# Inverse length-64 Fourier step as four 64x64 tiles from the second batch on

## The chip, the cores and the metric

The kernel runs on one core of a Trainium2 chip. The metric is the device time of one execution in microseconds; lower is better. The engines are named as in the profile: PE (TensorE: matmuls; its weight loads stand apart as PEld), DVE (VectorE), ACT (ScalarE), POOL (GpSimd) and SP (SyncE, which here only issues DMAs).

## The reference

Eight batches of 3008 rows (sequence) by 256 channels. First a filter in the frequency domain along the sequence, then an MLP mixer: over the sequence (tokens) and over the channels.

```python
X = np.fft.rfft(x, axis=1)                       # x: (8, 3008, 256)
y = np.fft.irfft(X * (filt_r + 1j * filt_i)[None], n=3008, axis=1)
h = np.maximum(y.transpose(0, 2, 1) @ w_tok1, 0.0) @ w_tok2   # 3008 -> 256 -> 3008
u = y + h.transpose(0, 2, 1)
out = u + np.maximum(u @ w_ch1, 0.0) @ w_ch2     # 256 -> 1536 -> 256
```

All data is fp32; the weights of the mixer arrive as float64 and are converted on the chip in the first part of the run.

## The kernel before

3008 is 47 x 64, and the length-3008 transform is done in two stages: one over the 64 rows that lie 47 apart, one over the 47. Rows n1 and -n1 are handled together (A = 24 pairs), so that each stage works with sums and differences. The first stage writes `z_tmp` to DRAM, the second reads it turned, multiplies with the filter and goes back over the 47, and leaves `g_tmp` in DRAM. What remains is the inverse over the 64: a product of each piece of `g_tmp` (tile `t4`, 128 partitions: 32 frequencies by 4 parts) with the constant table `wai` (128 x 128). This last step is not done by itself. It is accumulated into the same PSUM banks as the second token product, so that the bank holds u = y + h at once: `u_filter` (line 876) issues 4 matmuls of 128 columns with `t4` as the stationary operand and `wai` moving, for each half dh of the channels.

The mixer (`mix`) walks over items (b, m, jp): batch b, column block m (MT = 6 blocks of 512 sequence positions, the last of 448) and jp (JP = 6, pairs of 128 of the 1536 hidden channels). The two channel products, the second token product and, from the second batch on, the first token product use a Strassen-Winograd scheme: 7 products of half size in place of 8, with sums formed on DVE. A block of an item:

- place 0: `up_first` (L977: 4 matmuls into the two banks `ps_pg`), `up_middle` (DVE sums `hh` and `s`), `h_sums` of the item before (DVE `t`), part 0 of `down` (L1011), parts of the next u;
- place 1: `up_last` (L993: 3 matmuls; DVE `hh` twice, ACT relu twice), then up to two steps from the list `todo_v`;
- place 1.5 and 2: parts 1 and 2 of `down`, the steps of `finish` (DVE, then 16 output DMAs on POOL), parts of the next u.

The next block's u is made in four parts by `u_quarter` (L898 for the seven products, banks `ps_acc` and `ps_b` in turn): part 0 in item jp=2, part 1 at the begin of jp=3, parts 2 and 3 at its end; parts 2 and 3 begin with `u_filter`. Afterwards `v_steps` puts the channel sums (`v`: three DVE operations in two steps) into `todo_v`. For the first block of the next batch all of this lies in jp=4 and jp=5 of block m=5: parts 2 and 3 at place 0 of jp=5, the first two steps of `todo_v` at place 1, the rest at place 2. Batch 0 makes its u with `u_unit` and `u_filter`, with no Strassen scheme.

The forward filter of the next batch runs beside the mixer, at places that a table in the code fixes. From the third batch on it runs already as sets of four 64x64 matmuls (`four`, L528) on the four quarters of the array. DVE forms `sd` (x sums, L553), `p` (filter products, L709) and their join (L714, L715) for it.

The weights of the second token product, `w2`, lie in SBUF while batch 0 runs. `w2_sums` (POOL) forms the Strassen sums of each block during batch 0 and writes 7 matrices of 128 x 256 per block to `w2_tmp`; from batch 1 on `w2m_load` (SP) brings one block at a time back into one of two places.

The order on each engine is the order in which the code issues; nothing is rescheduled. Tiles with one or two buffers and the PSUM banks are what one engine waits for another for.

The lines that the steps below name:

```python
own = ({(3, 0): (0,), (3, 2): (1,)}, {(2, 2): (0,), (3, 0): (1,), (3, 2): (2, 3)})
new = {(JP - 2, 0): (0, 1), (JP - 1, 0): (2, 3)}
...
todo_v.extend(v_steps(b, m))
...
while todo_v and m + 1 == MT:
    one_step()
```

Of the kernel before, what the change touches and what calls it, by code (L numbers as in the profile page):

```python
# [59 lines left out]
def _make_tables():  # L60
# [12 lines left out]
    wa, wai = wa.reshape(P, P), wai.reshape(P, P)  # L73
# [51 lines left out]
    return wa.astype(f), np.concatenate((wa[one], wa[one])).astype(f), wa0.astype(f), wai.astype(f), wbi.astype(f), wbi0.astype(f)  # L125
# [3 lines left out]
def kernel(  # L129
# [13 lines left out]
    wa_np, was_np, wa0_np, wai_np, wbi_np, wbi0_np = _make_tables()  # L143
    wa_d = nc.inline_tensor(wa_np, name="wa_t").ap()
    was_d = nc.inline_tensor(was_np, name="was_t").ap()
    wai_d = nc.inline_tensor(wai_np, name="wai_t").ap()
    ident_d = nc.inline_tensor(np.eye(P, dtype=np.float32), name="ident_t").ap()
    wait_d = nc.inline_tensor(np.ascontiguousarray(wai_np.T), name="wait_t").ap()
# [7 lines left out]
                 for g, bs in enumerate(GROUPS)] for what, shape in (("z", (P, A)), ("g", (K2, KR))))  # L156

    w2_d = nc.dram_tensor("w2_tmp", (MT, P, 7, 256), FP32, kind="Internal").ap()
# [51 lines left out]
    w2m = [w2[:, t, 0:7 * 256].rearrange("p (s n) -> p s n", s=7) for t in range(2)]  # L210
# [145 lines left out]
    def w2_load(i):  # L356

        t, g = divmod(i, W2G)
        nn = min(NG, N2 - g * NG)
        n = nn * N1  # L360

        st = stage(512)
        nc.gpsimd.dma_start(st[:, 0:n], moe_w_tok2[ts(t, P), ds(g * NG * N1, n)])
        yield
        dst = w2[:, t].rearrange("p (a h n2) -> p h n2 a", h=2, n2=HALF)[:, :, ds(g * NG, nn), :]

        def some(h, first, step, w):
            return (lambda v: bass.AP(tensor=v.tensor, offset=v.offset + first, ap=[v.ap[0], [N1, nn], [step, w]]),
                    dst[:, h, :, 0:w])

        parts = [some(0, A - 1, -1, A), some(1, A, 1, A - 1)]
        if i < BY_PE:
            h = halves(st, n, spare_pair())
            yield next(h)
            yield next(h)
            on_chip(ident, *next(h), n, parts)
        else:
            yield from rounded(st, n, parts, False)
# [142 lines left out]
    def rows_of(t_d, b):  # L521
        g, i = place_of[b]
        return t_d[g].rearrange("k (g a) b d -> (k g) a b d", a=A)[:, :, i, :]
# [42 lines left out]
    def dft(bs):  # L566
# [109 lines left out]
        def bi_unit(k):  # L676


            ps = bank(free_bank()).rearrange("p (b d) -> p b d", b=2)[:, 0:nb, :]
            for i, p in enumerate(prods.pop(k)):  # L680
                wi = turn_i[:, k // WC % 4, k % WC] if i else wbs[k // WC][:, TI:TI + 2 * KR:2, k % WC]
                nc.tensor.matmul(ps[0:KR], wi, p, start=(i == 0), stop=(i == 1))
            c, r = divmod(k, KC)
            if r == 0:
                where, tag = (p2p, "p2") if c % 3 == 2 else (t3p, "t3")
                t3s[c] = where.tile([KR, KC, nb, D], FP32, tag=tag, name="t3")
            by_block(t3s[c][:, r], ps[0:KR])
            if r == KC - 1:
                nc.scalar.dma_start(g_d[0][ts(c, KC)].rearrange("k r b d -> r k b d"), t3s.pop(c))
# [27 lines left out]
        def bi_sets(c, tags):  # L717
# [7 lines left out]
            for h in range(2):  # L725
                nc.sync.dma_start(g_d[place_of[bs[0]][0]][ts(c, KD), ts(h, KH)].rearrange("k r b d -> r k (b d)"),
                                    t3[half_of(h, KH)])
# [53 lines left out]
    def t4_load(b, c, lo=PARTS[0], hi=P, queue=nc.sync):  # L781
        if lo == 0:
            t4[b, c] = t4p.tile([P, TC4, D], FP32, tag="t4", name="t4")
        queue.dma_start(t4[b, c][lo:hi], rows_of(g_d, b)[lo:hi, ts(c, TC4), :])
# [47 lines left out]
    def token_product(b):  # L832
# [20 lines left out]
        h1 = w2[:, 0:1, 7 * 256:].rearrange("p o (s t) -> p o s t", t=P)[:, :, 0:7, :]  # L853

        def finish_h1():
            v(c[:, 5:7], two[:, 1:3], c[:, 3:5])
            for at, to in ((slice(1, 7, 5), slice(0, 5, 4)), (slice(5, 8, 2), slice(1, 7, 5))):
                nc.scalar.activation(out=h1[:, 0, to, :], in_=c[:, at], func=AF.Relu)
# [29 lines left out]

    def u_quarter(b, m, h1, ut, i):

        w = width(m)
        hw = w // 2
        ps = bank(free_bank())
        if i >= 2:
            u_filter(b, m, i - 2, ps, True)
        todo = (((0, 0), (5, 3)), ((6, 4), (4, 6)), ((1, 1), (2, 2)), ((3, 5),))[i]
        for j, (n, at) in enumerate(todo):
            nc.tensor.matmul(ps[:, ds(j * hw, hw)], h1[:, n, :], w2m[m % 2][:, at, 0:hw],  # L898
                             start=(i < 2 and j == 0), stop=(j == len(todo) - 1))
        p0, p1 = ps[:, 0:hw], ps[:, hw:w]  # L900
        c11, c21, c22 = ut[:, 0, 0:hw], ut[:, 1, 0:hw], ut[:, 1, hw:w]
# [4 lines left out]
        elif i == 1:  # L906

            row = ut[:, 0, hw:w]
            both = bass.AP(tensor=row.tensor, offset=row.offset, ap=[row.ap[0], [512 - hw, 2], [1, hw]])
            v(both, ps[:, 0:w].rearrange("p (s n) -> p s n", s=2), c22.unsqueeze(1).to_broadcast([P, 2, hw]))  # L910
            v(c22, p0, c21)
        else:
            v(ut[:, i - 2, 0:w], ps[:, 0:w], ut[:, i - 2, 0:w])

    def w2m_load(m):
        hw = width(m) // 2
        nc.sync.dma_start(w2m[m % 2][:, :, 0:hw], w2_d[m, :, :, 0:hw])

    def w2_sums(m):

        w = width(m)
        hw = w // 2
        r = w2[:, :, ds(m * 512, w)]
        b11, b12, b21, b22 = (r[:, t, ds(j * hw, hw)] for t in range(2) for j in range(2))
        sub = lambda out, in0, in1: nc.gpsimd.tensor_tensor(out=out, in0=in0, in1=in1, op=ALU.subtract)

        def raw_out():
            nc.gpsimd.dma_start(w2_d[m, :, 0, 0:hw], b11)
            nc.gpsimd.dma_start(w2_d[m, :, 1:3, 0:hw], r[:, 1, :].rearrange("p (s n) -> p s n", s=2))

        def t13():
            sub(b22, b22, b12)
            sub(b12, b12, b11)

        def t24():
            nc.gpsimd.tensor_tensor(out=b11, in0=b22, in1=b11, op=ALU.add)
            sub(b21, b11, b21)

        def sums_out():
            for t in range(2):  # L940
                nc.gpsimd.dma_start(w2_d[m, :, ds(3 + 2 * t, 2), 0:hw], r[:, t, :].rearrange("p (s n) -> p s n", s=2))

        return [raw_out, t13, t24, sums_out]
# [70 lines left out]
    def store_piece(b, m, blocks, h, e, n, queues):  # L1014
        ob = out[b]
        cw = DH * CW
        row = e * 32 * N1 + (A + 4 * m if h else A - 1 - 4 * m)
        for g, q in enumerate(queues):
            q.dma_start(bass.AP(tensor=ob.tensor, offset=ob.offset + row * D + g * cw,  # L1019
                                ap=[[N1 * D, 32], [D if h else -D, n], [1, cw]]),  # L1020
                        blocks[ts(g, CW), h, e, 0:n])

    def last_item(b, m, jp, hh, t, ut, po):
# [29 lines left out]
        blocks = r.rearrange("p (q h e) d i -> p h e q (d i)", h=2, e=2)  # L1053
        for h in range(2):
            n = min(4, (w - h * HALF + HALF) // P)
            for e in range(2):
                for dh in range(DH):
                    rows = ut[:, dh].rearrange("p (q h e i) -> p h e q i", h=2, e=2, i=CW)
# [3 lines left out]
    def finish(b, m, ut, po):  # L1062
# [29 lines left out]
        def store():  # L1092
            turn(1)
            blocks = r.rearrange("p (q h e) d i -> p h e q (d i)", h=2, e=2)
# [30 lines left out]
    def mix(next_ready):  # L1125
# [14 lines left out]
        def u_parts(b, m, jp, place):  # L1140
# [5 lines left out]
            if now and now[-1] == max(p for ps in parts.values() for p in ps):  # L1146
                if m:
                    wait.append(m)
                todo_v.extend(v_steps(b, m))
# [92 lines left out]
    with tc.manual_schedule():  # L1242
        nc.sync.dma_start(wa0, wa0_d)
        nc.vector.memset(turned[:, A:K2, :], 0.0)
        for t in filts:
# [125 lines left out]
```

## Time and profile before

| | |
|---|---|
| median of 3 runs | 2401.5 us (2401.21 to 2401.79) |
| profiled execution: its span | 2400.3 us, so 1.2 us of the median lie around the span |
| PE busy | 2361.7 us, 98% |
| DVE busy | 1950.1 us, 81% |
| ACT busy | 689.6 us, 29% |
| POOL busy | 639.2 us, 27% |
| mean granted TensorE clock | 0.995 of full speed |
| DMA moved | 294.28 MB, mean 123 GB/s |

Busy time is the sum of the durations of an engine's instructions. Matmuls are pipelined: a row lasts longer than the distance to the next one, so for PE the starts of successive rows are what counts. DVE rows overlap a little as well. "Idle before, releaser" tells how long an engine stood idle ahead of a row and what ended this.

### The profile page before, as it was taken

The numbers are of one execution on the slowest core, as the hardware profiler recorded it, in microseconds if no ns is written. First come the engines' busy times: TensorE is split into PE (matmuls) and PEld (weight loads), VectorE is DVE, ScalarE is ACT, GpSimd is POOL, SyncE is SP. The second block draws the span as 40 slices with busy tenths as digits, with TensorE's granted clock in tenths as the row PEclk, the third lists the DMA queues.
The fourth block names the chain that finished last, engine by engine and source line by source line (L and its number), as shares of the span: only waits on it lengthen the run. The fifth ranks groups of instructions, "written<-read, shape, count | busy, mean of one in ns | idle before, by whom it ended". The sixth has DMA issues, their size and how long they took to land.

```text
span 2400.3 us, 37048 instructions
## 1 busy us (share of the span) xinstructions
PE 2361.7 (98%) x13132; PEld 2013.7 (84%) x13132; DVE 1950.1 (81%) x3669; ACT 689.6 (29%) x1339; POOL 639.2 (27%) x1124
## 2 busy tenths in 40 slices
PE   7989999999999999999999999999999999999998
PEld 4667788888898888988888888988889888898887
DVE  7798887788887888788887788788887788877786
ACT  5733222222223222232222222122222322212222
POOL 7475624211211121112111311221121112112121
PEclk8999999999999999999999999999999999999999
DMA  9964446333353333533344333533335433331100
GB/s 217 247 191 125 157 127 218 120 107 91 112 174 129 101 99 108 196 113 98 102 146 158 110 94 103 191 115 107 92 114 172 134 96 98 108 130 32 39 14 21
DMA packets 189719, 294.28 MB, mean 123 GB/s; under 512 B 34444, under 2 KB 124962, under 8 KB 189534
## 3 DMA queue, kind: packets, MB, share of 16 engines
q1 hardware_dynamic: 148046, 231.24, 30.8%
q0 software_dynamic: 34688, 53.83, 8.5%
q10 hardware_dynamic: 6800, 6.85, 0.9%
q8 instruction: 104, 1.70, 0.3%
q14 instruction: 81, 0.66, 0.1%
HBM read 209.06 MB, written 82.72 MB: 122 GB/s over the span
## 4 chain that ended last, share of the span: by engine, by line
PE 91%; DMA 3%; DVE 3%; POOL 1%; issue 1%; ACT 0%; SPq 0%; DVEq 0%; ACTq 0%; POOLq 0%
PE ps_po L1011 35%; PE ps_pg L977 19%; PE ps_pg L993 15%; PE ps_b L528 3%; PE ps_b L841 3%; PE ps_acc L898 3%; PE ps_acc L841 2%; PE ps_b L898 2%; PE ps_pg L528 2%; PE ps_b L876 2%; PE ps_acc L876 2%; PE ps_b L790 1%; DMA filt<-in_filt_r_dram 1%; DMA x<-in_x_dram 1%; DVE t L955 0%
## 5 line engine op out<-in xcount | busy, mean ns | idle before, releaser
L1019 POOL DMA_DIRECT2D out_dram<-r x752 | 408.3, 550 | 1454.0 <-issue 865.1
L998 ACT ACTIVATE hh<-hh 128x512 f32<-128x512 f32 (+1 forms) x576 | 347.9, 621 | 1015.8 <-DVE hh L955 1012.0
L955 DVE TENSOR_TENSOR hh<-ps_pg,s 128x512 f32<-128x512 f32 (+3 forms) x864 | 482.6, 586 | 168.1 <-ACT s L980 157.9
L1011 PE MATMUL ps_po<-t,wc 128*128 128x256 f32 (+1 forms) x2296 | 558.4, 380 | 0.8 <-DVE t L955 0.6
L1011 PEld LDWEIGHTS ps_po<-t,wc 128*128 128x128 f32 x2296 | 427.0, 190 | 96.4 <-issue 38.3
L977 PE MATMUL ps_pg<-v,wc 128*128 128x256 f32 (+1 forms) x1728 | 412.6, 375 | 0.1
L1011 PE MATMUL ps_po<-hh,wc 128*128 128x256 f32 (+1 forms) x1722 | 411.6, 375 | 0.6 <-POOL wc L387 0.6
L977 PEld LDWEIGHTS ps_pg<-v,wc 128*128 128x128 f32 x1728 | 328.2, 190 | 37.9 <-POOL wc L386 0.8
L1011 PEld LDWEIGHTS ps_po<-hh,wc 128*128 128x128 f32 x1722 | 327.1, 190 | 38.1 <-POOL wc L387 1.4
L993 PE MATMUL ps_pg<-u,wc 128*128 128x256 f32 (+1 forms) x1152 | 292.0, 376 | 3.1 <-DVE hh L955 2.9
L955 DVE TENSOR_TENSOR t<-t,hh 128x256 f32<-128x256 f32 (+1 forms) x576 | 246.7, 428 | 19.8
L993 PEld LDWEIGHTS ps_pg<-u,wc 128*128 128x128 f32 x1152 | 217.0, 190 | 35.0 <-DVE hh L955 9.3
L955 DVE TENSOR_TENSOR s<-ps_pg,hh 128x512 f32<-128x512 f32 (+1 forms) x288 | 196.1, 681 | 30.0
L980 ACT COPY s<-ps_pg 128x256 f32<-128x256 f32 (+1 forms) x288 | 105.9, 368 | 330.2 <-PE ps_pg L977 328.9
L955 DVE TENSOR_TENSOR t<-hh 128x512 f32<-128x512 f32 (+1 forms) x288 | 194.0, 674 | 0.6 <-ACT hh L998 0.6
L977 PE MATMUL ps_pg<-u,wc 128*128 128x256 f32 (+1 forms) x576 | 169.6, 376 | 4.2 <-DVE hh L955 4.2
L993 PE MATMUL ps_pg<-v,wc 128*128 128x256 f32 (+1 forms) x576 | 168.8, 375 | 0.0
L977 PEld LDWEIGHTS ps_pg<-u,wc 128*128 128x128 f32 x576 | 108.1, 190 | 20.4 <-DVE hh L955 8.4
L993 PEld LDWEIGHTS ps_pg<-v,wc 128*128 128x128 f32 x576 | 108.9, 190 | 12.9
L955 DVE TENSOR_TENSOR u<-ps_acc,u 128x256 f32<-128x256 f32 (+1 forms) x84 | 46.2, 550 | 72.4 <-PE ps_acc L898 50.0
L955 DVE TENSOR_TENSOR u<-ps_b,u 128x512 f32<-128x512 f32 (+2 forms) x126 | 74.5, 591 | 28.9 <-PE ps_b L898 26.7
L898 PE MATMUL ps_acc<-w 128*128 128x256 f32 (+1 forms) x336 | 85.2, 376 | 0.0
(164 smaller groups left out, 2692.3 us busy)
## 6 DMA issues: line engine op xcount, KB each, us to landing
w<-w_tmp SPq DMA_DIRECT2D x84, 448.0 KB
w<-w_tmp SPq DMA_DIRECT2D x35, 896.0 KB
out_dram<-r POOLq DMA_DIRECT2D x696, 32.0 KB, 3.3
g_tmp<-t SPq DMA_DIRECT2D x112, 192.0 KB
t<-g_tmp SPq DMA_DIRECT2D x42, 512.0 KB
t<-z_tmp SPq DMA_DIRECT2D x196, 96.0 KB
z_tmp<-t SPq DMA_DIRECT2D x72, 256.0 KB
wb<-wbi_t SPq DMA_DIRECT2D x56, 256.0 KB
```

Of the source, the lines that this page charges most:

```text
L528: nc.tensor.matmul(outs(i, j), stat(i, j), mov(i, j), start=True, stop=True)
L790: nc.tensor.matmul(acc[:, t, :], w1[:, a, ts(t, P)], t4[b, a // TC4][:, a % TC4, :], start=(a == 0 and t == 0), stop=(a == A - 1 and t == ...
L841: nc.tensor.matmul(ps[:, at], w[:, n], mov, start=(j == 0 and i in (0, 2)), stop=(j == AP - 1 and i >= 5))
L876: nc.tensor.matmul(ps[:, ds(q * P, n)], t4[b, c][:, r, ts(dh, P)], wai[:, 0:n], start=(first and q == 0), stop=(not first and q == 3))
L898: nc.tensor.matmul(ps[:, ds(j * hw, hw)], h1[:, n, :], w2m[m % 2][:, at, 0:hw], start=(i < 2 and j == 0), stop=(j == len(todo) - 1))
L955: nc.vector.tensor_tensor(out=out, in0=in0, in1=in1, op=op)
L977: nc.tensor.matmul(ps[:, 0:hw], chan[0][:, jp, n, :], mov, start=True, stop=True)
L980: nc.scalar.copy(out=s[:, 0], in_=g[0][:, 0, 0:hw])
L993: nc.tensor.matmul(ps[:, 0:hw], chan[0][:, jp, n, :], mov, start=True, stop=True)
L998: nc.scalar.activation(out=hs, in_=hs, func=AF.Relu)
L1011: nc.tensor.matmul(po[i][:, j, 0:hw], chan[1][:, jp, n, :], mov, start=(jp == 0 and first == 1), stop=(jp == JP - 1 and last == 1))
L1019: q.dma_start(bass.AP(tensor=ob.tensor, offset=ob.offset + row * D + g * cw, ap=[[N1 * D, 32], [D if h else -D, n], [1, cw]]), blocks[ts(g ...
```

## The change

From batch 1 on, the inverse step over the 64 is split by the parity of the frequency parts. Half of the partitions of `t4` now hold the parts that give the sum of output rows n2 and 63 - n2 (plus), the other half those that give their difference (minus). Each is a 64x64 table, and a set of four tiles (two halves of `t4` by two halves of 128 channels) makes both at once, with 64 moving columns: `u_sets` issues 32 matmuls of 64x64x64 per block, all ahead of the last three Strassen products. Plus goes to one PSUM bank, minus to the other. Part 3 of the u is empty now, part 2 has three products.

Since the products of the token weights are added to the same banks, the weights need the same form: `w2_sums` first turns each pair of columns into half sum and difference (six more POOL operations per block; the scale 0.5 is in the relu), and `w2_tmp` now holds four rows of 512 columns per block, the three duplicates left in. All Strassen products have 256 columns, at m=5 too. After the evacuation, `u_turn` forms plus + minus and plus - minus in place on DVE (two steps in `todo_v`, ahead of `v_steps`). The columns of a block are then ordered by row half first, and the second half of rows is in reversed order, so the output DMAs of that half change their pattern. `g_tmp` is laid out by half, so batch 0's writes and partial reloads of it come in two DMAs each.

```diff
-    wa, wai = wa.reshape(P, P), wai.reshape(P, P)
+    by_half = wai.reshape(K2, 2, 2, P).transpose(1, 0, 2, 3).reshape(P, P)
+    wa, wait = wa.reshape(P, P), by_half.T
+    wai = np.concatenate((by_half[:, one], by_half[:, two][:, ::-1]), axis=1)
...
-                 for g, bs in enumerate(GROUPS)] for what, shape in (("z", (P, A)), ("g", (K2, KR))))
-    w2_d = nc.dram_tensor("w2_tmp", (MT, P, 7, 256), FP32, kind="Internal").ap()
+                 for g, bs in enumerate(GROUPS)] for what, shape in (("z", (P, A)), ("g", (2, K2, KH))))
+    w2_d = nc.dram_tensor("w2_tmp", (MT, P, 4, 512), FP32, kind="Internal").ap()
...
-                nc.scalar.dma_start(g_d[0][ts(c, KC)].rearrange("k r b d -> r k b d"), t3s.pop(c))
+                t3 = t3s.pop(c)
+                for h in range(2):
+                    nc.scalar.dma_start(g_d[0][h, ts(c, KC)].rearrange("k r b d -> r k b d"), t3[ts(h, KH)])
...
-        queue.dma_start(t4[b, c][lo:hi], rows_of(g_d, b)[lo:hi, ts(c, TC4), :])
+        for to in [slice(lo, hi)] if hi - lo == P else [slice(h * HALF + lo // 2, h * HALF + hi // 2) for h in range(2)]:
+            queue.dma_start(t4[b, c][to], rows_of(g_d, b)[to, ts(c, TC4), :])
...
-                nc.scalar.activation(out=h1[:, 0, to, :], in_=c[:, at], func=AF.Relu)
+                nc.scalar.activation(out=h1[:, 0, to, :], in_=c[:, at], func=AF.Relu, scale=0.5)
...
+    def u_sets(b, m, pss):
+        for dh in range(DH):
+            for q in range(4):
+                c, r = divmod(4 * m + q, TC4)
+                for e in range(2):
+                    for i in range(2):
+                        nc.tensor.matmul(pss[e][half_of(i), dh, ts(q, HALF)],
+                                         t4[b, c][half_of(e), r, ds(dh * P + i * HALF, HALF)], wai[half_of(e), 0:HALF],
+                                         start=(dh == 0 and q == 0), stop=False)
...
     def u_quarter(b, m, h1, ut, i):
-        w = width(m)
-        hw = w // 2
-        ps = bank(free_bank())
-        if i >= 2:
-            u_filter(b, m, i - 2, ps, True)
-        todo = (((0, 0), (5, 3)), ((6, 4), (4, 6)), ((1, 1), (2, 2)), ((3, 5),))[i]
-        for j, (n, at) in enumerate(todo):
-            nc.tensor.matmul(ps[:, ds(j * hw, hw)], h1[:, n, :], w2m[m % 2][:, at, 0:hw],
-                             start=(i < 2 and j == 0), stop=(j == len(todo) - 1))
+        todo = (((0, 0), (5, 3)), ((6, 4), (4, 6)), ((1, 1), (2, 2), (3, 5)), ())[i]
+        if not todo:
+            return
+        pss = [bank(free_bank()).rearrange("p (s n) -> p s n", s=2) for _ in range(1 + (i == 2))]
+        if i == 2:
+            u_sets(b, m, pss)
+            places = (pss[0][:, 0], pss[1][:, 0], pss[0][:, 1])
+        else:
+            places = (pss[0][:, 0], pss[0][:, 1])
+        for j, ((n, at), to) in enumerate(zip(todo, places)):
+            nc.tensor.matmul(to, h1[:, n, :], w2_at(m, at), start=(i < 2 and j == 0), stop=(j >= 1))
...
-            v(ut[:, i - 2, 0:w], ps[:, 0:w], ut[:, i - 2, 0:w])
+            for e in range(2):
+                v(us[:, :, e], pss[e], us[:, :, e])
+
+    def u_turn(ut):
+        us = ut.rearrange("p d (e n) -> p d e n", e=2)
+        plus, minus = us[:, :, 0], us[:, :, 1]
+
+        def first():
+            v(plus, plus, minus)
+
+        def second():
+            nc.vector.scalar_tensor_tensor(out=minus, in0=minus, scalar=-2.0, in1=plus, op0=ALU.mult, op1=ALU.add)
+
+        return [first, second]
...
-        nc.sync.dma_start(w2m[m % 2][:, :, 0:hw], w2_d[m, :, :, 0:hw])
+        nc.sync.dma_start(w2m[m % 2], w2_d[m])
...
+        def turn_out():
+            for t in range(2):
+                pool(halves_of[:, t, 1], halves_of[:, t, 0], halves_of[:, t, 1])
+                pool(halves_of[:, t, 0], halves_of[:, t, 0], halves_of[:, t, 0], ALU.add)
+                pool(halves_of[:, t, 0], halves_of[:, t, 0], halves_of[:, t, 1])
+            nc.gpsimd.dma_start(w2_d[m, :, 0:2], r)
...
-        row = e * 32 * N1 + (A + 4 * m if h else A - 1 - 4 * m)
-        for g, q in enumerate(queues):
-            q.dma_start(bass.AP(tensor=ob.tensor, offset=ob.offset + row * D + g * cw,
-                                ap=[[N1 * D, 32], [D if h else -D, n], [1, cw]]),
-                        blocks[ts(g, CW), h, e, 0:n])
+        row = (HALF - 1 - e * 32) * N1 + A + 4 * m if h else e * 32 * N1 + A - 1 - 4 * m
+        for i, q in enumerate(queues[0:n] if h else queues):
+            if h:
+                to, ap, of = (row + i) * D, [[cw, CB], [-N1 * D, 32]], blocks[:, h, e, i]
+            else:
+                to, ap, of = row * D + i * cw, [[N1 * D, 32], [-D, n]], blocks[ts(i, CW), h, e, 0:n]
+            q.dma_start(bass.AP(tensor=ob.tensor, offset=ob.offset + to, ap=ap + [[1, cw]]), of)
...
+                if b:
+                    todo_v.extend(u_turn(uts[b, m]))
                 todo_v.extend(v_steps(b, m))
...
+        nc.gpsimd.memset(w2[:, :, A * P - HALF:], 0.0)
```

## The prediction

> **What bounds the kernel now.** I read the page's busy table and the chain of waits first, then TensorE's timeline in the stretch that the change replaces, then an existing burst of 64x64 tiles, then the seam between two batches on both engines.
>
> ```profile
> PE 2361.7 (98%) x13132; PEld 2013.7 (84%) x13132; DVE 1950.1 (81%) x3669; ACT 689.6 (29%) x1339; POOL 639.2 (27%) x1124
> PE 91%; DMA 3%; DVE 3%; POOL 1%; issue 1%; ACT 0%; SPq 0%; DVEq 0%; ACTq 0%; POOLq 0%
> ```
>
> 91% of the chain is TensorE; DMA, DVE and POOL lie on it almost only in the first 140 us. From the second batch on, a microsecond taken from TensorE is a microsecond of the span, unless DVE is then late. DVE has room on average (81%), so its order in time decides.
>
> The stretch that changes (TensorE; start us, length us, line, out<-in, count). Every fp32 matmul shows as two rows of the count:
>
> ```profile
> 1086.57 1.05 PE L876 MATMUL ps_acc<-wai,t 128*128 128x128 f32 x8
> 1087.46 1.03 PE L898 MATMUL ps_acc<-w 128*128 128x256 f32 x4
> 1088.33 1.05 PE L876 MATMUL ps_b<-wai,t 128*128 128x128 f32 x8
> 1089.22 0.60 PE L898 MATMUL ps_b<-w 128*128 128x256 f32 x2
> 1089.65 0.59 PE L977 MATMUL ps_pg<-u,wc 128*128 128x256 f32 x2
> ```
>
> From start to start, the inverse step (L876) takes 0.89 + 0.89 = 1.78 us per column block m: 16 rows at 0.111 us. The 256-column rows pace at 0.216 us.
>
> An existing tile burst, and what surrounds it:
>
> ```profile
> 1001.89 0.73 PE L1011 MATMUL ps_po<-t,wc 128*128 128x224 f32 x3
> 1002.55 0.65 PE L528 MATMUL ps_b<-sd,was 64*64 64x512 f32 x2
> 1002.57 0.65 PE L528 MATMUL ps_acc<-sd,was 64*64 64x512 f32 x2
> 1003.03 0.60 PE L528 MATMUL ps_b<-sd,was 64*64 64x512 f32 x2
> 1003.05 0.59 PE L528 MATMUL ps_acc<-sd,was 64*64 64x512 f32 x2
> 1003.57 1.02 PE L1011 MATMUL ps_po<-t,wc 128*128 128x224 f32 x4
> ```
>
> Four tiles start within 0.02 us and run side by side: 512 columns cost 0.429 us a pass. The third 224-column row before it starts at 1002.27 and would be through at 1002.46; the four rows after it last 1.02 us instead of the usual 0.92, so the way back is complete at 1003.67. 1.21 us less two passes of 0.43 leaves **0.35 us for going into tiles and back**. The bursts of four and eight passes of 256 columns give 0.35 and 0.36: it is a price per burst, whatever its length.
>
> **The change, part by part** (against the profiled span 2400.3; the times' median is 2401.5, so 1.2 us lie around the span).
>
> *Inverse step.* It happens 7 batches x 6 m = 42 times. The 8 full-array matmuls become 8 rounds of four 64x64 tiles with 64 columns: 32 matmuls, 64 rows, 16 passes. No row shows a 64-column pass. Below, it can't beat streaming, 64 x 0.429/512 = 0.054 us; and a 64-column weight load is followed by the next one in the same tile 0.055 us later (single rows of the burst above: 1002.553, 1002.608). Above, load and stream one after the other make 0.109. I take 0.056, half the 0.112 between 128-column loads in L876, because those are the nearest rows, and loads and streams overlap there. Issue can keep up: in the burst above the pairs of load and matmul start 0.007 us apart, and four per pass is 0.028. So 16 x 0.056 + 0.35 = 1.25 us, a gain of 0.53. At m=5, whose last piece has 64 columns, the old step takes 1.68, gain 0.43. 35 x 0.53 + 7 x 0.43 = **-21.5 us**.
>
> A rule speaks against this. The single rows show a weight load for a tile starting 0.002 us after a matmul began in that tile (1025.901 after 1025.899), and the next matmul exactly 0.429 us later, so the load was hidden.
> The Trainium skill ("TensorE: Matmul & The Clock Gate", Part 3, what overlaps) says that a load overlaps running matmuls only when its row group differs; by it nothing would be hidden, the step would take about 2.1 us (an estimate) and the kernel would end near 2436 us; I go by the row.
>
> *Width.* The seven Strassen products of m=5 now have 256 columns, not 224: 7 x 2 rows x (0.216 - 0.189) = 0.38, in 7 batches **+2.6 us**.
>
> *DVE.* Two new 128x512 operations per m turn sum and difference back (42 x 2; rows of this size 0.69 us, a scalar_tensor_tensor 0.72): 59 us of DVE, and one more step before the channel sums (v). Evacuation keeps its count, but now both PSUM reads come behind the last product instead of one before it. Inside a batch the new pair takes the place of v in item jp=4, and v goes to jp=5. There up_last starts at 1100.80 and the DVE pair hh at 1101.96 (0.60 apart); v then starts at 1103.16 instead of the filter's join. v's second operation comes 0.72 after its first (1095.02, 1095.74), lasts 0.42 and is seen 0.06 later: 1104.36. The next item's second matmul, which reads it, started at 1104.26. So +0.10 us, 35 times: **+3.5 us**. The join behind v makes DVE some 0.5 us late in the next item; the nearest reader there (first half of down, jp=1) keeps 0.02 us of slack by the same counting, so I take 0 and keep up to 0.1 x 35 for the range.
>
> *Seam between batches.* Here the parts come at jp=5 and all four steps must be through before the next batch's first item. Batch 6 to 7, both engines:
>
> ```profile
> 2148.24 0.92 PE L993 MATMUL ps_pg<-u,wc 128*128 128x224 f32 x4
> 2148.44 0.69 DVE L955 TENSOR_TENSOR u<-ps_b,u 128x512 f32<-128x512 f32 x1 [0.63 <-PE ps_b L898]
> 2149.20 1.15 DVE L955 TENSOR_TENSOR hh<-ps_pg,s 128x448 f32<-128x448 f32 x2
> 2150.27 0.68 DVE L955 TENSOR_TENSOR v<-u 128x512 f32<-128x512 f32 x1
> 2150.89 0.59 PE L977 MATMUL ps_pg<-u,wc 128*128 128x256 f32 x2
> 2150.98 0.88 DVE L955 TENSOR_TENSOR v<-v,u 128x256 f32<-128x256 f32 x2
> 2151.46 1.56 PE L977 MATMUL ps_pg<-v,wc 128*128 128x256 f32 x6
> ```
>
> The last line already waits for v (v starts 2150.98, +0.42, +0.06). Counted from up_last (2148.24 = 0), DVE then does: two evacuations at 0.20 and 0.80, hh at 1.40 and 1.94, the two turns at 2.48 and 3.20, v at 3.92 and 4.64; it is seen at 5.12, where the matmul now starts at 3.22. Queued behind that matmul is all of TensorE's next item: 1.9 us lost. At the other six seams two x sums lie between turns and v, v is seen at 6.20, and the matmul now starts at 4.30: again 1.9. 7 x 1.9 = **+13.3 us**. Should the second evacuation and the turns overlap better, 1.45 is the low end.
>
> *Start.* The first batch's filter output leaves in two DMAs on ACT's queue, and its last reload comes in two per tile on SP and POOL. Both stand on the chain (103.95, 4.48 us; 108.50, 2.30 us). One more issue each is 0.31 (ACT) and 0.42 (SP); POOL's memset ahead of the first x loads is some 0.2: **+1 us**, 0 to +3 if other waits on DMA semaphores appear.
>
> *Second token weights.* POOL gets 36 more 128x256 operations (0.83 each, 30 us) in batch 0 and 12 fewer DMA issues (0.55). It then idles 12 us and more ahead of most stores, and the weights are read two items later at the soonest. DVE rows with two SBUF inputs that overlap a POOL addition took 0.86 instead of 0.43 us (11 of 480), behind TensorE's cover. 0, up to +3. The bigger loads (1 MB for 0.9) and the reordered stores (as many issues, one fewer per edge at m=5) run beside DMA at 3 to 4 tenths, and POOL at 27%: 0; without that cover a load's 0.1 MB at the 123 GB/s shown is 1 us.
>
> **Sum**: -21.5 + 2.6 + 3.5 + 13.3 + 1 = -1.1, so 2400.4 us. What this measurement can tell from no change is 0.2%, 4.8 us.
>
> **Rivals.** *Loads not hidden in the tiles (slower).* If a pass costs 0.109, the step is 16 x 0.109 + 0.35 = 2.09; against 1.25 that is 42 x 0.84 = +35, 2436. It decides from 0.089 a pass, where the old 1.78 is reached. Against it is the row above; for it, that no row loads four tiles' weights in every pass. *The seams are covered (faster).* If TensorE has other work there, or DVE's operations overlap, the 13.3 falls away: 2387. For it: only seven places; against: the last line above already waits. *DVE falls behind inside the batches (slower).* Another 0.25 us per m, 42 x 0.25 = +10, 2411. For it: jp=1 and jp=5 hold 8.2 and 6.4 us of DVE rows in 8.1 and 6.0 us; against: rows overlap by 0.09 and jp=3 has over 2 us free. That the tiles don't run side by side is nearly excluded by the burst.
>
> **How the numbers follow.** My sum 0.60, hidden seams 0.15, loads not hidden 0.15, DVE behind 0.10. Its own ends: passes at 0.054, seams at 1.45, nothing inside batches or at the start give -23.1 + 2.6 + 10.2 = -10 (2391); passes at 0.062, 0.2 inside batches, start and POOL at 3 each give -17.7 + 2.6 + 13.3 + 7 + 6 = +11 (2413). The range 2386 to 2416 takes in the hidden seams and DVE behind, and leaves out the unhidden loads. Of my sum's 0.60, some 0.36 lies within 4.8 us, 0.14 below, 0.10 above. With the rivals: faster 0.29, same 0.36, slower 0.35.
>
> **What would show it.** Tile matmuls on ps_acc and ps_b of 64x64 by 64, passes 0.056 apart, 1.25 us from start to start around them; a TensorE wait for v of about 2 us at seven seams and 0.1 elsewhere; DVE near 2009 us. A pass at 0.09 or more, or seams without a wait, proves me wrong.

## The result, and the profile after

The changed kernel takes 2429.4 us (median of 4 runs, 2427.4 to 2433.0), against 2401.6 for the kernel before beside it: a ratio of 1.0109, 95% interval 1.0093 to 1.0125. I had forecast 2400.4, with 2416 as the upper end. The profiled span grew by 25.4 us, from 2400.3 to 2425.7.

The page after, first its busy row, then the shares of the chain of waits (they add up to 87%: the chain was followed back to about 302 us only, so it says nothing of the start):

```profile
PE 2366.4 (98%) x15148; PEld 1979.3 (82%) x15148; DVE 2006.1 (83%) x3753; ACT 689.4 (28%) x1339; POOL 708.8 (29%) x1138
PE 84%; DVE 3%; issue 0%; ACT 0%; DVEq 0%; ACTq 0%
```

Busy time does not show the loss: PE stays at 98%, and DVE came out as forecast (2009). So I took the first matmul of every item as a mark (L1019, before L977) and compared the 288 item times of the two traces, which from batch 1 on agree to 0.01 us where nothing changed. The column "my sum" sorts the terms of the prediction by place. In us, against the kernel before:

| stretch | my sum | after | e9 | e12 |
|---|---|---|---|---|
| until the first item | +1 | +11.7 | +11.1 | -0.9 |
| items jp=3 of blocks m=0 to 4, batches 1 to 7 (tiles, width of m=5) | -15.2 | -15.6 | -15.5 | -15.5 |
| seven seams (last two items of a batch, first two of the next), tiles there included | +9.6 | +12.5 | -2.7 | -2.5 |
| other items of batches 1 to 7 | +3.5 | +9.8 | +1.7 | +1.2 |
| batch 0 without its seam | 0 | +5.4 | +6.4 | +6.5 |
| after the last matmul | 0 | +1.6 | +1.6 | +1.3 |
| span | -1.1 | +25.4 | +2.6 | -10.1 |

(e9 and e12 are mended kernels from below.) Part of the width of m=5 falls outside its row: it makes item jp=2 of block m=4 0.11 us longer, 0.8 us in all, which stands under the other items.

*The tiles.* PE's timeline around one burst in the changed kernel (start us, length, line, out<-in, count):

```profile
1024.80 1.11 PE L1053 MATMUL ps_po<-hh,wc 128*128 128x224 f32 x5
1025.84 0.27 PE L904 MATMUL ps_acc<-wai,t 64*64 64x64 f32 x2
1025.86 0.27 PE L904 MATMUL ps_b<-wai,t 64*64 64x64 f32 x2
1025.95 0.23 PE L904 MATMUL ps_acc<-wai,t 64*64 64x64 f32 x2
...
1026.93 0.70 PE L924 MATMUL ps_acc<-w 128*128 128x256 f32 x2
1027.47 0.59 PE L924 MATMUL ps_b<-w 128*128 128x256 f32 x2
```

Passes come 0.058 us apart (1025.95 to 1026.01 and on). From where the work before is through (1025.75) to where the 256-column rows are back at their pace, 1.29 us go by, for the 1.25 of my sum; the old step took 1.78. An item jp=3 fell from 9.99 to 9.49 us (in block m=4 from 9.72).

*The seam*, DVE and then PE, batch 6 to 7:

```profile
2169.85 0.69 DVE L997 TENSOR_TENSOR u<-ps_acc,u 128x512 f32<-128x512 f32 x1 [1.53 <-PE ps_acc L924]
2170.46 0.68 DVE L997 TENSOR_TENSOR u<-ps_b,u 128x512 f32<-128x512 f32 x1
2171.06 1.14 DVE L997 TENSOR_TENSOR hh<-ps_pg,s 128x448 f32<-128x448 f32 x2
2172.12 0.68 DVE L997 TENSOR_TENSOR u<-u 128x512 f32<-128x512 f32 x1
2172.83 0.69 DVE L950 SCALAR_TENSOR_TENSOR u<-u 128x512 f32<-128x512 f32 x1
2173.56 0.69 DVE L997 TENSOR_TENSOR v<-u 128x512 f32<-128x512 f32 x1
2174.28 0.88 DVE L997 TENSOR_TENSOR v<-v,u 128x256 f32<-128x256 f32 x2
```

```profile
2172.95 0.67 PE L1019 MATMUL ps_pg<-u,wc 128*128 128x256 f32 x2 [0.48 <-DVE u L997]
2174.76 2.47 PE L1019 MATMUL ps_pg<-v,wc 128*128 128x256 f32 x6 [1.15 <-DVE v L997]
```

It is the chain that I had counted: evacuation, hh, two turns, v. PE stands at two places now, for the first turn and for v.

*Inside the batches*, PE where the item after jp=5 begins, before (the view ends after four of six rows) and after, and the weight loads after:

```profile
1103.82 0.60 PE L977 MATMUL ps_pg<-u,wc 128*128 128x256 f32 x2
1104.26 1.03 PE L977 MATMUL ps_pg<-v,wc 128*128 128x256 f32 x4
```

```profile
1123.20 0.59 PE L1019 MATMUL ps_pg<-u,wc 128*128 128x256 f32 x2
1123.73 1.56 PE L1019 MATMUL ps_pg<-v,wc 128*128 128x256 f32 x6
```

```profile
1123.73 0.94 PEld L1019 LDWEIGHTS ps_pg<-v,wc 128*128 128x128 f32 x5 [0.34 <-DVE v L997]
```

The matmul that reads v starts 0.53 us after the item's first, not 0.43: the 0.10 us that I had forecast. But the six rows last 1.56 in place of 1.46: it is the weight load that waits for v, so the load begins with the matmul and nothing hides it (that matmul lasts 483 ns, its neighbours 379). Being late by 0.10 us cost the item 0.20 to 0.21.

*The start*, PE's timeline before, then after:

```profile
99.79 0.61 PE L668 MATMUL ps_pg<-turned,wb 128*128 128x256 f32 x2
110.93 13.36 PE L790 MATMUL ps_b<-t,w 128*128 128x256 f32 x53 [2.28 <-DMA t<-g_tmp]
```

```profile
106.01 0.61 PE L674 MATMUL ps_pg<-turned,wb 128*128 128x256 f32 x2
121.46 2.90 PE L799 MATMUL ps_b<-t,w 128*128 128x256 f32 x6 [5.44 <-DMA t<-g_tmp]
```

The last step of the loop over the 32 frequencies (L674) starts its last row at 106.2 where it did at 100.0, and the first token product (L799) starts at 121.5, not 110.9, after a wait of 5.4 us (before 2.3) for a reload of `g_tmp`. That is 10.5 us of the 11.7. The other 1.2 us agree with the granted TensorE clock: over the 10 us from the first token product on it was 0.71 here and 0.83 before.

*Batch 0*, at the same item: DVE and POOL before, then DVE and POOL after:

```profile
257.69 0.89 DVE L955 TENSOR_TENSOR t<-t,hh 128x256 f32<-128x256 f32 x2
255.03 2.07 POOL L804 TENSOR_TENSOR w<-w 128x384 f32<-128x384 f32 x2
```

```profile
270.73 1.97 DVE L997 TENSOR_TENSOR t<-t,hh 128x256 f32<-128x256 f32 x2
```

```profile
269.13 2.42 POOL L813 TENSOR_TENSOR w<-w 128x384 f32<-128x384 f32 x2
271.60 1.69 POOL L965 TENSOR_TENSOR w<-w 128x256 f32<-128x256 f32 x2
```

Before, POOL has ended (257.10) when DVE's sums begin. After, it adds beside them (L965 is the turn and the sums of the second token weights), and DVE's sums of two SBUF operands take about twice as long, so that t comes late for down. Of the 70 sums into t of this kind in batch 0, 21 last over 0.6 us, before 7, and all 28 ran beside a POOL addition.

### The profile page after: what moved, and what is told of

Read it like the earlier page. It is cut to its first block, busy times and chain, and to the rows that moved or that the text cites. A ratio compares the mean times of both kernels' runs of the same rounds, so it can differ in the third digit from the quotient of the medians.

```text
span 2425.7 us, 41188 instructions
## 1 busy us (share of the span) xinstructions
PE 2366.4 (98%) x15148; PEld 1979.3 (82%) x15148; DVE 2006.1 (83%) x3753; ACT 689.4 (28%) x1339; POOL 708.8 (29%) x1138
## 4 chain that ended last, share of the span: by engine, by line
PE 84%; DVE 3%; issue 0%; ACT 0%; DVEq 0%; ACTq 0%
PE ps_po L1053 33%; PE ps_pg L1019 19%; PE ps_pg L1035 14%; PE ps_acc L924 3%; PE ps_b L850 3%; PE ps_b L534 3%; PE ps_acc L850 2%; PE ps_pg L534 2%; PE ps_b L924 2%; PE ps_acc L904 2%; DVE u L997 1%; DVE hh L997 1%; DVE t L997 1%; DVE v L997 0%; PE ps_b L904 0%
## 5 line engine op out<-in xcount | busy, mean ns | idle before, releaser
L1065 POOL DMA_DIRECT2D out_dram<-r x738 | 453.2, 624 | 1386.1 <-issue 991.5
L1019 PE MATMUL ps_pg<-v,wc 128*128 128x256 f32 (+1 forms) x1728 | 419.0, 379 | 11.6 <-DVE v L997 11.6
L1019 PEld LDWEIGHTS ps_pg<-v,wc 128*128 128x128 f32 x1728 | 325.7, 191 | 61.6 <-DVE v L997 25.4
L1019 PE MATMUL ps_pg<-u,wc 128*128 128x256 f32 (+1 forms) x576 | 169.7, 376 | 4.4 <-DVE hh L997 4.0
L1035 PE MATMUL ps_pg<-v,wc 128*128 128x256 f32 (+1 forms) x576 | 168.8, 375 | 0.0
L997 DVE TENSOR_TENSOR u<-ps_acc,u 128x256 f32<-128x256 f32 x84 | 46.8, 557 | 109.3 <-PE ps_acc L924 85.9
L1019 PEld LDWEIGHTS ps_pg<-u,wc 128*128 128x128 f32 x576 | 107.8, 190 | 22.0 <-DVE hh L997 8.5
L1035 PEld LDWEIGHTS ps_pg<-v,wc 128*128 128x128 f32 x576 | 108.7, 190 | 13.3 <-DVE s L997 0.4
L924 PE MATMUL ps_acc<-w 128*128 128x256 f32 x336 | 97.5, 392 | 0.0
L717 DVE TENSOR_TENSOR p<-ps_b,filt 128x1024 f32<-128x1024 f32 x56 | 68.4, 1222 | 14.2 <-PE ps_pg L534 13.3
```

Of the source, the lines that this page charges most:

```text
L717: nc.vector.tensor_tensor(out=prods[c, h], in0=pss[h].unsqueeze(1).to_broadcast([P, 2, 2, D]), in1=filts[c % FB], op=ALU.mult)
L924: nc.tensor.matmul(to, h1[:, n, :], w2_at(m, at), start=(i < 2 and j == 0), stop=(j >= 1))
L997: nc.vector.tensor_tensor(out=out, in0=in0, in1=in1, op=op)
L1019: nc.tensor.matmul(ps[:, 0:hw], chan[0][:, jp, n, :], mov, start=True, stop=True)
L1035: nc.tensor.matmul(ps[:, 0:hw], chan[0][:, jp, n, :], mov, start=True, stop=True)
L1065: q.dma_start(bass.AP(tensor=ob.tensor, offset=ob.offset + to, ap=ap + [[1, cw]]), of)
```

## Experiments

Theory: the tiles gain what was forecast, and five separate losses eat it: the split of `g_tmp` at the start, v late at the seams, v late inside batches, POOL against DVE in batch 0, the stores at the end. The rival: one shared cause, more work on DVE and the queues than the kernel can hide, so that a mend in one place only moves the wait.

All are timed against the kernel before beside them (2402.9 to 2403.7 us). The profiled first item of six kernels with the same start (the changed one, e3, e4, e7, e8, e9) lies between 152.5 and 157.5 us, so edits elsewhere are read from the item times, and a first item from one profile has that spread.

**e2: the split of g_tmp alone, in the kernel before.** As in the change: two writes per pair of frequencies, two DMAs per partial reload, rows of the tables to match.

```diff
-    ... ("g", (K2, KR))
+    ... ("g", (2, K2, KH))
...
-    wa, wai = wa.reshape(P, P), wai.reshape(P, P)
+    by_half = wai.reshape(K2, 2, 2, P).transpose(1, 0, 2, 3).reshape(P, P)
+    wa, wai = wa.reshape(P, P), np.ascontiguousarray(by_half)
```

> The kernel before, with only g_tmp laid out by half: two writes per pair of frequencies on ACT in batch 0, two DMAs per partial reload, tables with their rows in the new order. No tiles, no turn, old weights. Theory (the whole loss of the start comes from this split): the first mixer item moves from 141.4 to about 153 us and the time from 2401.6 to 2412 to 2414. Rival (the split is worth about 1 us, as I had predicted, and the start is late through POOL's memset, the weights or the new tables): 2402 to 2404.

2415.0 us, ratio 1.0047 (1.0034 to 1.0060), 11.3 us above the kernel before beside it; first item at 152.9. The whole loss of the start is the split; POOL's memset, weights and tables have no share in it.

**e13 and e14: the two halves of the split, each alone in the kernel before.**

```diff
-                nc.scalar.dma_start(g_d[0][ts(c, KC)]..., t3s.pop(c))
+                t3 = t3s.pop(c)
+                for h in range(2):
+                    nc.scalar.dma_start(g_d[0][ts(c, KC), ts(h, KH)]..., t3[ts(h, KH)])
```

```diff
-        queue.dma_start(t4[b, c][lo:hi], ...)
+        for to in [slice(lo, hi)] if hi - lo == P else [slice(lo, (lo + hi) // 2), slice((lo + hi) // 2, hi)]:
+            queue.dma_start(t4[b, c][to], ...)
```

> The kernel before, with batch 0's g_tmp written in two DMAs per pair of frequencies (48 partitions each) into the same places; reloads, order and tables untouched. Theory (ACT bounds that loop; 16 more issues at 0.31 to 0.39 us and dearer ones are 6 to 7 us): the loop over the frequencies ends at 106 to 107 us in place of 100.0, the first mixer item comes at 147 to 149 in place of 141.4, 2408 to 2410. Rival (ACT has slack, and the reloads carry the 11.3 us that the split cost): loop and first item late by under 2 us, 2402 to 2404.

> The kernel before, with each of batch 0's 24 partial reloads of g_tmp in two DMAs (halves of its rows); writes, order and tables untouched. Theory (the rest of the start's loss, some 4 to 5 us, is SP and POOL issuing twice as many reloads behind the last write): the loop ends at 100 us as before, the first token product starts 3 to 5 us later than at 110.9, 2405 to 2407. Rival (the reloads alone are covered, and the 4 us come only when the writes are late too): under 1.5 us, 2401 to 2403.

e13: 2407.8, ratio 1.0021 (1.0012 to 1.0029). e14: 2410.0, ratio 1.0031 (1.0019 to 1.0043). PE's timeline of e13, then of e14:

```profile
105.63 0.61 PE L668 MATMUL ps_pg<-turned,wb 128*128 128x256 f32 x2
...
116.62 7.58 PE L792 MATMUL ps_b<-t,w 128*128 128x256 f32 x34 [0.62 <-issue]
```

```profile
99.96 0.61 PE L668 MATMUL ps_pg<-turned,wb 128*128 128x256 f32 x2
...
117.23 7.11 PE L791 MATMUL ps_b<-t,w 128*128 128x256 f32 x22 [8.42 <-DMA t<-g_tmp]
```

Doubled writes lengthen the loop (105.8 for 100.0) and leave the gap behind it as it was (10.8 us, before 10.9); ACT's `g_tmp` issues in it went from 16 x 0.315 = 5.0 to 32 x 0.407 = 13.0 us. Busy time does not tell whose loop it is: in the kernel before, PE's rows fill it (61.97 us of the 62 from 38 to 100), and ACT's rows and issues cover 4.2 us of the 4.4 that a pair of frequencies takes. The run does: 0.50 us more of issues on ACT per pair made the pair 0.48 us longer (4.86 for 4.38). It is ACT's loop.

Doubled reloads leave the loop alone (100.2) and lengthen the gap by 6.3 us. In the chain of waits the last piece ahead of the first token product is issued at 110.85 (before 108.50), because SP issues the pieces one after the other, about 0.34 us each, and it lands 6.27 us later (before 2.30). So 2.3 us are SP's issuing and 4.0 a slower landing. POOL issued its 470 KB loads of token weights from 109.5 here, ahead of that piece, and from 110.6 before, behind it; from 112 to 117 us POOL's queue held 92% of the DMA engines' time and SP's 9%. That these loads delay the piece is read from the trace; no run moved them.

First items at 145.4 and 148.1: +4.0 and +6.7, together 10.7 of the 11.5 of e2. By the medians it is 4.9 and 7.1, together 12.0 of 11.3. In e13 the first token product was 5.7 us late, and 1.7 of it came back because the clock over the next 10 us was 1.00, not 0.83. The writes cost less than expected, the reloads more.

**e5: one write per pair, reloads still split**, in the changed kernel.

```diff
+            v0 = g_d[0].rearrange("k (h g a) b d -> h k g a (b d)", h=2, a=A)
+            for h in range(2):
+                queue.dma_start(t4[b, c][h * HALF + lo // 2:h * HALF + hi // 2],
+                                v0[h, lo // 4:hi // 4, :, ts(c, TC4)])
```

> The changed kernel; batch 0's g_tmp keeps the old order in DRAM, so that each pair of frequencies leaves in one DMA again (16 issues on ACT), while every reload still comes in two DMAs, one per half. Splitting g_tmp by itself cost the kernel before 11.3 us; this run parts that into writes and reloads. Theory (ACT bounds batch 0's filter loop): the 16 added issues and the dearer issue, 7.4 us of ACT, go away, so the first mixer item starts at 145 to 146 us in place of 153.1 and the time is about 2422. Rival (the doubled reloads hold the loop up): first item at 151 us or later, 2427 to 2429.

2428.8, ratio 1.0108 (1.0094 to 1.0122). The loop ends at 99.4 again, yet the first token product comes at 121.6. The reloads now read two runs per frequency, and their issue on SP rose from 0.346 to 0.614 us (42 of them, 25.8 us): another queue took the place of ACT. It couldn't tell the two halves apart, which is why e13 and e14 were made.

**e10: reloads in three steps of rows, not four** (36 DMAs, their places in the loop moved to suit).

```diff
-PARTS = (0, 64, 96, 112)
+PARTS = (0, 96, 112)
```

> The changed kernel, batch 0's g_tmp reloaded in three steps of rows (0 to 96, 96 to 112, the rest) in place of four: 36 DMAs, not 48; the writes stay doubled. Theory (after the last write SP and POOL still have some 22 reload DMAs to issue at 0.34 us and more, which holds the first token product up): the loop over the frequencies still ends at about 106 us, but the token product starts 2 to 4 us sooner than at 121.5; 2425 to 2427. Rival (the wait is for the last write's data, not for the issue of the pieces): start unchanged within 0.7 us, 2429.

2428.0, ratio 1.0103 (1.0088 to 1.0119); token product at 121.7: a miss, as the rival had it. SP stands waiting for the late writes until 112.8 and then still has 18 pieces to issue, 6.3 us (16 after 113.4 in the changed kernel); the saved ones were not those at the end.

**e6 and e11: batch 0 in the old order altogether.** One write, one DMA per partial reload, the old row order in `wai` until batch 1. The first token weights must then change their order for batch 1: in e6 by two DMAs per load, in e11 by four copies in DRAM (shown here).

```diff
+        old = w1_d.rearrange("j (k h g) s n -> h g j k (s n)", h=2, g=2)
+        new = w1p_d.rearrange("j (h k g) s n -> h g j k (s n)", h=2, g=2)
+
+        def turn_rows(h, g):
+            return lambda: nc.gpsimd.dma_start(new[h, g], old[h, g])
```

> The changed kernel; batch 0 keeps the old order of g_tmp, of t4 and of its table altogether (one write per pair, one DMA per partial reload, the old row order in wai until batch 1 needs the new one; the first token weights then come in two DMAs per load from batch 1 on). Theory: the start is as before the change, first mixer item at 141 to 142 us, time 2417 to 2419. Rival (part of the start's loss is POOL's memset, the turned token weights or other tables): first item at 144 us or later.

> Batch 0 in the old order of rows again, but the first token weights are put into the new order once, by four copies from DRAM to DRAM on POOL's queue in batch 0, so that each load stays one DMA. Theory: the start keeps its 139.7 to 141.5 us, and the batches are as in the changed kernel (307.9, 285.5, ...): 2416 to 2419. Rival (the copies, 5.5 MB, hold up stores or loads in batch 0): batch 0 at 311 us or more, 2421 or more.

e6: first item at 139.7, but 2431.5, ratio 1.0117 (1.0103 to 1.0131): the item with the token product of batch 1 took 32.2 us in place of 24.2, and items of later batches near it grew too, with the loads of its weights doubled. e11: 2414.7, ratio 1.0046 (1.0034 to 1.0059), first item at 141.8, batch 0 at 307.8. The start is won back whole.

**e3: at the seam, parts 2 and 3 at the end of jp=4.** All four DVE steps then stand at place 1 of jp=5.

```diff
-        new = {(JP - 2, 0): (0, 1), (JP - 1, 0): (2, 3)}
+        new = {(JP - 2, 0): (0, 1), (JP - 2, 2): (2, 3)}
...
+                while todo_v and now and jp == JP - 1 and m + 1 == MT:
+                    one_step()
```

> The changed kernel, with the tiles and the last three token products for the first block of the next batch at the end of item jp=4 of m=5 in place of the begin of jp=5, and all four DVE steps after them (two turns, two of v) at place 1 of jp=5. Theory (v is late at the seam only because DVE gets evacuation, hh, turn and v in one row): the first item of batches 1 to 6 falls from 7.67 to about 5.7 us and that of batch 7 from 8.85 to about 6: -12 to -15, 2414 to 2417. Rival (the parts then stand behind the banks and DVE's work of item jp=4, so that the wait moves there): under 5 us won, and jp=4 or jp=5 of m=5 longer by about as much as jp=0 is shorter.

2423.9, ratio 1.0083 (1.0069 to 1.0097). jp=0 fell from 7.67 to 6.36 only, and jp=1 rose from 8.69 to 9.01; the seven seams won 6.5 us of the 16. The turns still stood behind hh: at one seam DVE idled 3.2 us ahead of the evacuation and then worked without a pause until v.

**e4: inside the batches, parts 2 and 3 behind up_last of jp=3, turns at its end.**

```diff
-        ... (3, 2): (2, 3)})
+        ... (3, 1): (2, 3)})
...
+            if now and b and m + 1 < MT:
+                u_parts(b, m, jp, 1)
...
+                if b and jp == 3 and m + 1 < MT:
+                    one_step()
+                    one_step()
```

> The changed kernel, inside the batches: the tiles and the last three token products at place 1 of item jp=3 in place of its end, and the two turns on DVE at the end of jp=3, where DVE has over 2 us free, so that v is formed in jp=4 again as before the change. Seams untouched. Theory (jp=0 and jp=1 grew by 0.21 and 0.12 us because v and the join behind it come one item later): jp=0 goes from 6.25 back to 6.04 and jp=1 from 8.26 to 8.13, 35 x 0.21 + some 20 x 0.12 = -9 to -10, 2419 to 2421. Rival (DVE's total work is the limit, wherever the turns stand): jp=4 or jp=5 grow by as much, 0 to -3.

2428.0, ratio 1.0102 (1.0089 to 1.0116). jp=0 and jp=1 came back to 6.04 and 8.13, but jp=3 rose from 9.49 to 9.67: the tiles came so early that those of `ps_b` waited 0.20 us for part 1's evacuation. A half miss, and it suggested placing them one step later.

**e7: parts 2 and 3 between parts 1 and 2 of down, turns straight behind them.**

```diff
-        ... (3, 2): (2, 3)})
+        ... (3, 1.5): (2, 3)})
-        new = {(JP - 2, 0): (0, 1), (JP - 1, 0): (2, 3)}
+        new = {(JP - 2, 0): (0, 1), (JP - 2, 1.5): (2, 3)}
...
+            if now:
+                u_parts(b, m, jp, 1.5)
...
-                    "e": ((4, 1.5), (5, 1.5))
+                    "e": ((4, 2), (5, 1.5))
...
+                if jp == (JP - 2 if m + 1 == MT else 3) and (b or m + 1 == MT):
+                    one_step()
+                    one_step()
```

> The changed kernel; the tiles and the last three token products stand between part 1 and part 2 of down (item jp=3 inside a batch, jp=4 of block m=5 at the seam), the two turns on DVE directly after them, and the filter's tile step of jp=4 behind part 2. DVE then has both turns in time in which it idled, and v comes where it came before. Theory (all lateness inside batches and at the seams is DVE's queue behind a late evacuation): jp=0 back to 6.04, jp=1 to 8.13, the seam's jp=0 from 7.67 to about 5.7 and batch 7's from 8.85 to about 6: some 10 inside batches and 15 at the seams, 2404 to 2407. Rival (the lateness moves on, as in the two earlier shifts, which gave back 0.18 us per block in jp=3 and 0.27 per seam in jp=4): at best half, 2415 to 2418.

2419.8, ratio 1.0071 (1.0059 to 1.0084). Inside the batches all came true: 6.04, 8.13, 9.49. At the seams v was in time, and other things were not. PE's waits from batch 1 on, and ACT's row at one seam:

```profile
PE ps_pg L1035 <- DVE hh L997: 4.7, 5, 1.5
PE ps_b L534 <- DVE u L997: 3.6, 5, 0.7
```

```profile
1037.91 0.59 ACT L550 COPY t<-ps_b 128x512 f32<-128x512 f32 x1 [3.42 <-DMA z_tmp<-t]
```

The filter's tiles (L534) waited for the banks, and ACT waited 3.4 us for a write of `z_tmp`, which held its copy s and with it hh. My reading was that the write was queued behind the 1 MB load of token weights.

**e9: the seam cleared.** Against e7:

```diff
-                    "e": ((4, 2), (5, 1.5))
+                    "e": ((5, 0), (5, 2))
...
-                    w2m_load((m + 2) % MT)
+                    (late_load.append if m == 0 else w2m_load)((m + 2) % MT)
...
+                if late_load and jp == 0:
+                    w2m_load(late_load.pop())
```

> The run with all parts earlier, and two more edits at the seam: the filter's two tile steps of block m=5 stand in item jp=5 (behind part 0 of down, and at the end) in place of jp=4 and jp=5, and the 1 MB load of token weights that followed the last part at once is issued in the next item. Theory (what the earlier parts gave back at the seams is PE waiting for the banks of the filter's tiles, and ACT waiting 3 us for a z_tmp write queued behind the 1 MB load): jp=4 of m=5 falls from 11.5 to about 10.85, jp=0 of the next batch from 5.7 to 7.4 to a steady 5.7, jp=1 from 9.4 to 8.7; the seams are then all won, 2404 to 2407. Rival (DVE's and ACT's own work fills these items): each seam keeps 1 us or more, 2411 or more.

2405.3, ratio 1.0009 (1.0000 to 1.0018). Five of the seven seams take 0.56 us less than before the change, one 0.27 less, the last 0.4 more. DVE at one of them, and PE's waits from batch 1 on, as the view lists them:

```profile
1299.72 0.69 DVE L997 TENSOR_TENSOR u<-ps_acc,u 128x512 f32<-128x512 f32 x1 [0.99 <-PE ps_acc L924]
1300.32 0.68 DVE L997 TENSOR_TENSOR u<-ps_b,u 128x512 f32<-128x512 f32 x1
1301.04 0.69 DVE L997 TENSOR_TENSOR u<-u 128x512 f32<-128x512 f32 x1
1301.77 0.69 DVE L950 SCALAR_TENSOR_TENSOR u<-u 128x512 f32<-128x512 f32 x1
```

```profile
PE ps_pg L1019 <- DVE v L997: 0.8, 1, 0.8
PE ps_po L1074 <- ACT hh L1040: 0.2, 1, 0.2
```

The turns follow the evacuation at once, and of 9.8 us of waits for v 0.8 are left (batch 6 to 7). Which of the two edits freed the `z_tmp` write was not parted.

**e8: without POOL's turn of the second token weights**; the kernel leaves that part of the computation out.

```diff
-            for t in range(2):
-                pool(halves_of[:, t, 1], halves_of[:, t, 0], halves_of[:, t, 1])
-                pool(halves_of[:, t, 0], halves_of[:, t, 0], halves_of[:, t, 0], ALU.add)
-                pool(halves_of[:, t, 0], halves_of[:, t, 0], halves_of[:, t, 1])
```

> The changed kernel without the six POOL operations per block that turn the second token weights into half sums and differences; that part of the computation is left out. Theory (batch 0 is 5 us longer because POOL's additions slow DVE's sums from 0.43 to 0.83 us where both run at once): batch 0 falls from 307.9 to about 303 us, 2424 to 2425. Rival (it is longer because the stores' issues on POOL went from 550 to 624 ns): batch 0 stays above 306.5, 2428 to 2430.

2425.3, ratio 1.0088 (1.0075 to 1.0102). Batch 0 fell from 307.9 to 304.6 (308.8 in other kernels with the same batch 0), and as before the change 7 of the 70 sums are slowed. So the turn costs 3 to 4 us of the 5.4 to 6.4 by which batch 0 is longer. What is left is within the spread of batch 0 among kernels that do not change it (302.8 to 304.6 in the kernel before, e2, e13 and e14).

**e12: all mends**: e9 and e11, and in the last item

```diff
-        for h in range(2):
+        for h in (1, 0):
...
-                store_piece(b, m, blocks, h, e, n, (nc.sync, nc.scalar) * 2)
+                store_piece(b, m, blocks, h, e, n, ((nc.sync, nc.scalar), (nc.scalar, nc.sync))[e] * 2)
```

> All mends together: batch 0 in the old order with the copies, parts and turns earlier, the seam cleared, and in the last item the row-wise stores first and spread evenly over SP and ACT. If the losses are separate and add up: 2429.4 - 11.7 (start) - 10 (inside the batches) - 14 (seams) - 1 (end) = 2393, 0.3 to 0.45% below the kernel before; POOL's added work in batch 0 stays. If the losses share a cause or DVE and the DMA queues fill up: above 2400.

2394.6 us (2392.0 to 2395.7), ratio 0.9960 (0.9948 to 0.9973): 0.4% below the kernel before and 35 us below the changed one. The gains of e9 (24) and e11 (15) add up to 39 us, and 35 were measured; in the profiled spans the two give 34.5 and e12 35.6. So the losses were separate in the main and the rival falls. At the end only 0.3 of 1.6 us came back: the row-wise stores of the second half take 0.54 to 0.65 us per issue (one on ACT 1.4), the others some 0.43, in either order.

## Why the prediction was wrong, step by step

- **Inverse step and width: right.** 1.29 us for 1.25, passes at 0.058 for 0.056; -15.6 in jp=3, +0.8 in jp=2 and 7 x -0.5 at the seams make -18.3, my two terms -18.9. The row on hidden weight loads held. The Trainium skill ("TensorE: Matmul & The Clock Gate", Part 3) lets a load overlap running matmuls only when its row group differs; my estimate by it, with nothing hidden, was 2.1 us for the step, and the measurement decides against that here.
- **Start: the step that failed.** I read which instruction stood last on the chain and charged one more issue on each queue, +1, "0 to +3". The split doubled 16 writes and 24 reloads, and all of them counted. ACT set the pace of the whole loop, so that 16 x 0.31 on ACT alone is 5 us (the loop grew by 6.2). Behind the last write SP's doubled issues cost 2.3 us in e14, and the landing behind POOL's loads 4.0. The start measured +11.7, 10.7 of the 26.5 us between my sum and the span. The Trainium skill ("Perfetto Trace Analysis", DMA Optimizations) says that splitting DMAs may let a task end sooner if the DMA engines are generally idle. Here they were busy for 0.93 of the time from 38 to 100 us in the kernel before and 0.73 from 96 to 111, and in e13 and e14 the first item came 4.0 and 6.7 us later.
- **DVE inside the batches: half.** The lateness of 0.10 us was right, the price of a wait was not: 0.20 to 0.21, for the exposed weight load. jp=1, which I took at 0 with 0.02 us of slack, lost 0.12 in about half of the blocks. Without the width it is +9.0 for +3.5. The rival "DVE falls behind" (+10) has the number by luck: it blamed too much DVE work per m, and e7 got the time back with the same work in another order.
- **Seams: right in mechanism, a little small.** Without the tiles' share +16.0 for +13.3: 2.0 us at six of them, 3.6 at the last in the profiled run. In e5, e6, e8, e10 and e11 the last seam, unchanged, lost 1.9.
- **Second token weights: at 0, the wrong end.** I had 0, up to +3; it measured +5.4, of which e8 gives the turn 3 to 4. The row that I cited (DVE 0.86 for 0.43 beside POOL) was the cause; PE's cover did not hold for all 21 sums.
- **Stores at 0: right inside, not at the end**, where nothing hides the dearer issues: +1.6.
- **The rivals.** Unhidden loads and covered seams did not happen. No rival joined several small losses, so 2416 was too low an upper end.

## What to carry to other kernels

When a change doubles DMAs, multiply every one of them by its issue time on its queue, and ask for each stretch whether that queue sets the pace there, even if it is idle over the whole run. Ask too which large loads of another queue then come ahead of the late pieces. An operand that was late for a matmul cost the lateness and its weight load too. Work that makes an operand late can often be moved to where its engine idles: here the same instructions in another order gave back 24 of the 28 us by which the kernel had become slower.

## What I had not expected of the hardware

- The issue of a DMA of batch 0's `g_tmp` on ACT took 0.315 us alone and on average 0.39 to 0.42 in pairs; on SP a reload with two runs per frequency took 0.61 for 0.35.
- Tiles whose weights change with every pass of 64 columns still pass every 0.058 us in four at once, and into and out of tiles takes 0.36 us, as with long passes.
- The granted clock in the 10 us behind the first token product was 0.83 before, 0.71 after, 0.78 in e14, 1.00 in e13 and e12, and the time from there to the first item (30.5, 31.6, 30.9, 28.8 and 28.8 us) was within 0.1 us of 28.8 plus ten times what the clock lacked of full speed. The length of the wait in front does not fix it alone: 2.3 us before, 2.8 in e12.
